# Routing the row tiles of a fused retention and mixture-of-experts kernel in groups of six instead of four or five

## The chip, the cores and the metric

The kernel runs on one core of one Trainium2 chip. The time is that of one execution on the device, in microseconds. The core has a matrix engine (TensorE, PE), a vector engine (VectorE, DVE), an activation engine (ScalarE, ACT), GpSimd (POOL) and a queue engine (SyncE, SP). Each works through its own instructions in order, and they wait for each other through semaphores.

## The reference, cut to what matters

```python
scores = (1/8) * q @ k.T                     # 8 batches x 8 heads x 576 x 64
x = (scores * decay_mask) @ v                # -> 4608 rows of 512
# first mixture layer
logits = x @ w_gate
e_idx  = argmax(logits, axis=1)              # one of 8 experts for each row
gate_w = softmax(logits)[e_idx]
eom    = sigmoid(x @ w_output_gate)[e_idx]
y[row] = gate_w * eom * (relu(x @ w1[e_idx]) @ w2[e_idx])
# second mixture layer: the same on y, with a bias by modality in the logits and no eom
```

## The kernel before, in words

The kernel has two parts. The first part (`attention_and_routing`, up to about 283 us of the profiled execution) computes the retention and the routing of the first mixture layer. The second part (`experts`, the rest) runs both expert layers; no line of it is touched.

The 4608 rows are cut into 36 row tiles of 128 rows. Nine tiles belong to a pair of batches: four chunks of each batch, and a "tail" tile (the ninth) made of the last 64 rows of both. Each tile is an object `Chunk` with some 30 parts: splits of q, k and v into a high and a low half (lines 308 to 341), scores (line 343), masks on POOL or DVE (line 360), the state of the recurrence (lines 371 to 390), products with the state (`qS`, line 407) and with v (`av`, line 425), the scaled output (`out`, line 429), the sum of squares (line 433), scales from its exponent (`row_scale` and `row_scale2`, lines 440 to 446), the row in two halves (lines 448 to 453), its DMA transpose (line 455), and the logits (line 457), which PE writes for each tile into its own 64 columns of a PSUM bank that the group shares.

The routing is done once for a group of tiles, in the generator `route` (line 207): a chain of small DVE instructions over all tiles of the group (sum of the logits' three parts, the product with the scale `iv`, maximum, one-hot choice `oh`, running counts `pre`, softmax denominators, positions `pi`), with two exponentials on ACT and two matmuls on PE between them. One step of the generator is issued at a time. After the last step `scatter` (line 201) writes each tile's rows to DRAM with an indirect DMA that POOL issues. The groups before are the tiles 0 to 3, 4 to 8, 9 to 12, 13 to 17, 18 to 21, 22 to 26, 27 to 30, 31 to 34 and 35: nine groups, eight of four or five tiles and one of a single tile.

The order of the work is written out by hand. Each part of tile i has a due time i + `PLAN[part]` in units of a tile (about 7 us in the middle of this part). The steps of a group's `route` follow the due time of its last logits at 0.1684 units each, its scatters come 0.225 units after the last step and 0.428 units apart, and 16 conversions of the first expert's weights (line 545, one ACT and one DVE instruction each) are due at the times in `WEIGHTS`. All of it is sorted by due time, and that is the order of each engine's instructions. Due times say nothing of the real time: an engine starts its next instruction when what it waits for is there.

Where the last group's chain has its place is read from the same numbers: its last logits are due at 34 + 5.707 = 39.707, its 21 steps end at 43.243, and the single tile's chain ends at 44.257. Weight conversions are due at 39.36, 39.38, 39.68, 39.83, 43.38, 44.04, 44.13, 45.14 and later.

The first part ends with a drain (the trace puts it on line 1434): SP waits for the scatters' data to land, and then all engines go on to the experts.

Of the kernel before, what the change touches and what calls it, by code (L numbers as in the profile page):

```python
# [11 lines left out]
F16 = mybir.dt.float16  # L12
BF16 = mybir.dt.bfloat16
F32 = mybir.dt.float32
I32 = mybir.dt.int32
AF = mybir.ActivationFunctionType
ALU = mybir.AluOpType
AX = mybir.AxisListType

B, H, S, HD = 8, 8, 576, 64  # L20
D, F, E = 512, 1024, 8
N = B * S
P = 128
# [4 lines left out]
XW = 512 + XM  # L28
# [4 lines left out]
NT = N // P  # L33
# [21 lines left out]
    "mh1": (1.231, 1.362, 1.017, 0.873, 1.420),  # L55
    "ml1": (1.412, 1.539, 1.052, 1.300, 1.605),
    "av1": (2.106, 1.795, 1.790, 1.802, 2.282),
    "qS1": (-8.214, 2.045, 1.567, 1.937, 1.514),
    "out": (2.400, 2.098, 1.999, 2.210, 2.465),
    "sq": (2.541, 2.150, 3.296, 2.949, 2.775),  # L60
    "rs1": (2.976, 2.479, 3.923, 3.559, 3.293),
# [6 lines left out]
FIRST = -3.462, -0.341, 0.344, 0.159, -0.039  # L68
GATES = -5.2, -1.440, -2.415, 1.091
WARM = 15  # L70
STEPS, STEP, LATE, SLACK = 21, 0.1684, 14, 1
SCATTER = 0.225, 0.428
WEIGHTS = 39.36, 39.38, 39.68, 39.83, 43.38, 44.04, 44.13, 45.14, 52.52, 59.82, 70.32, 70.53, 71.67, 73.74, 109.54, 132.91

# [36 lines left out]
def attention_and_routing(tc, st, I, K):  # L111
# [3 lines left out]
    one, two, three = pool("one", 1), pool("two", 2), pool("three", 3)  # L115
# [72 lines left out]
    class Group:  # L188


        def __init__(self, start, items):
            self.tag, self.items, self.G, self.start = start, items, len(items), start
            tag = start
            for i, x in enumerate(items):
                x.group, x.place = self, i
            s1 = lambda n, dt=F32: two.tile([P, 5], dt, bufs=3, tag=n, name=f"{n}{tag}")
            self.ss, self.eb, self.sc, self.iv = s1("ss"), s1("eb", I32), s1("sc"), s1("iv")
            self.xrow = two.tile([P, 5, XW], F32, bufs=3, tag="xr", name=f"xr{tag}")
            self.pm = None

    def scatter(x):
# [5 lines left out]
    def route(gr):  # L207

        v, G, tag, pm, sc, iv = nc.vector, gr.G, gr.tag, gr.pm, gr.sc, gr.iv
        sm = lambda w, n, dt=F32: two.tile([P, 5, w], dt, tag=n, name=f"{n}{tag}")  # L210
        s1 = lambda n, dt=F32: two.tile([P, 5], dt, tag=n, name=f"{n}{tag}")
        g = slice(0, G)
        bc = lambda a, w: a[:, g].unsqueeze(2).to_broadcast([P, G, w])
        lg, dl, ex, wq, oh = sm(16, "lg"), sm(8, "dl"), sm(8, "ex"), sm(8, "wq"), sm(8, "oh", F16)
        mx, se, m2 = s1("mx"), s1("se"), s1("m2")
        v.tensor_reduce(lg[:, g], pm[:, 0:64 * G].rearrange("p (g c) -> p g c", c=64)[:, :, 0:48].rearrange("p g (s e) -> p g e s", s=3), axis=AX.X, op=ALU.add)
        yield
        v.tensor_tensor(lg[:, g], lg[:, g], bc(iv, 16), op=ALU.mult)
        yield
        v.tensor_reduce(mx[:, g], lg[:, g, 0:8], axis=AX.X, op=ALU.max)  # L220
        yield
        v.tensor_tensor(dl[:, g], lg[:, g, 0:8], bc(mx, 8), op=ALU.subtract)
        yield
        desc = col("desc").unsqueeze(1).to_broadcast([P, G, 8])
        v.scalar_tensor_tensor(wq[:, g], dl[:, g], 0.0, desc, op0=ALU.is_ge, op1=ALU.mult)
        yield
        v.tensor_reduce(m2[:, g], wq[:, g], axis=AX.X, op=ALU.max)
        yield
        v.tensor_tensor(oh[:, g], wq[:, g], bc(m2, 8), op=ALU.is_ge)
        nc.scalar.activation(ex[:, g], dl[:, g], AF.Exp)  # L230
        yield

        pre = two.tile([P, 6, 8], F16, tag="pre", name=f"pre{tag}")
        v.tensor_copy(pre[:, 0], cum[0])
        for t in range(5):
            if t < G:
                v.tensor_tensor(pre[:, t + 1], pre[:, t], oh[:, t], op=ALU.add)
            yield
        cum[0] = pre[:, G]
        zz, pr = sm(8, "zz"), sm(8, "pr")  # L240
        z, en, pf, pi = s1("z"), s1("en"), s1("pf"), s1("pi", I32)
        v.tensor_tensor(zz[:, g], lg[:, g, 8:16], oh[:, g], op=ALU.mult)
        yield
        v.tensor_reduce(z[:, g], zz[:, g], axis=AX.X, op=ALU.add)
        yield
        v.tensor_reduce(se[:, g], ex[:, g], axis=AX.X, op=ALU.add)

        o = pm[:, 320:320 + 8 * G]
        nc.tensor.matmul(o, tri, oh[:, g, :], start=True, stop=False)
        nc.tensor.matmul(o, ones, pre[:, g, :], start=False, stop=True)  # L250
        yield
        v.tensor_scalar(se[:, g], se[:, g], 1e-9, None, op0=ALU.add)
        nc.scalar.activation(en[:, g], z[:, g], AF.Exp, scale=-1.0)
        yield
        meta = gr.xrow[:, g, 512:XW]
        t0 = gr.items[0].row
        v.tensor_copy(meta[:, :, 1:XM], tokm[:, t0:t0 + G, :])
        yield
        v.tensor_tensor(pr[:, g], o.rearrange("p (g e) -> p g e", e=8), oh[:, g], op=ALU.mult)
        yield  # L260
        v.tensor_reduce(pf[:, g], pr[:, g], axis=AX.X, op=ALU.add)
        yield

        v.scalar_tensor_tensor(en[:, g], en[:, g], 1.0, se[:, g], op0=ALU.add, op1=ALU.mult)
        yield
        v.tensor_copy(pi[:, g], pf[:, g])
        v.scalar_tensor_tensor(meta[:, :, 0], en[:, g], WS * WS, sc[:, g], op0=ALU.mult, op1=ALU.mult)
        gr.pi = pi
# [16 lines left out]
    class Chunk:  # L285
# [74 lines left out]
        def mask(self, r, part):  # L360

            src = (self.au, self.al)[part][r]
            dst = src if part else three.tile([P, 512], F16, bufs=3, tag="ah", name=f"ah{self.tag}_{r}")
            self.aa[r][part] = dst
            s4, d4 = (t_.rearrange("p (h i) -> p h i", h=4) for t_ in (src, dst))
            if self.tail or self.on(("mh1", "ml1")[part]) is nc.vector:
                nc.vector.tensor_tensor(d4, s4, self.causal(), op=ALU.mult)
            else:
                nc.gpsimd.affine_select(out=d4, in_=s4, pattern=[[0, 4], [1, C]], compare_op=ALU.is_ge, fill=0.0, base=0, channel_multiplier=-1)
# [73 lines left out]
        def row_scale2(self):  # L443
            v = nc.vector
            v.tensor_scalar(self.of("sc").bitcast(I32), self.of("eb"), -8388608.0, 195.0 * 8388608.0, op0=ALU.mult, op1=ALU.add)
            v.tensor_scalar(self.of("iv").bitcast(I32), self.of("eb"), 8388608.0, 59.0 * 8388608.0, op0=ALU.mult, op1=ALU.add)

        def x_hi(self):
            self.xr = self.group.xrow[:, self.place, 0:512].bitcast(F16)
# [16 lines left out]
        order += [Chunk(2 * bp + bb, c) for bb in range(2) for c in range(NCH)] + [Chunk(2 * bp, NCH)]  # L466
    for i, x in enumerate(order):
        x.before = [order[i - 5], order[i - 1]] if x.tail else [order[i - 1]] if x.c else []
    cuts = [0] + [x + 9 * bp for bp in range(B // 2) for x in (4, 9)]
    cuts.insert(-1, NT - 1)  # L470
    groups = [Group(a, order[a:z]) for a, z in zip(cuts, cuts[1:])]
    whole = lambda f: lambda x: None if x.tail else f(x)
    parts = {
# [24 lines left out]
    for gr in groups:  # L498
        last = max(gr.start + n + PLAN["lg"][x.c] for n, x in enumerate(gr.items))
        chain = route(gr)  # L500
        for k in range(STEPS):
            last += STEP if k != LATE else STEP * SLACK
            add(last, next, chain, None)
        for n, x in enumerate(gr.items):
            add(last + SCATTER[0] + n * SCATTER[1], scatter, x)
# [13 lines left out]
    pm = ps.tile([P, 512], F32, tag="pl", bufs=2, name="pm_cnt")  # L519
# [901 lines left out]
def build(nc, I, off, outs):  # L1421
    with ExitStack() as st:
        sb = lambda n, s, dt: st.enter_context(nc.sbuf_tensor(n, s, dt))[:]
        K = {"off": off}
        K["cst"] = sb("cst", [P, max(b for _, b in off.values())], F32)
        K["ones"], K["tri"] = sb("ones", [P, P], F16), sb("tri", [P, P], F16)
        K["wg2"] = sb("wg2", [P, 4, 24], BF16)
        K["bias"] = sb("bias", [P, 16], F32)
        K["reg1"] = sb("reg1", [1, 24], I32)
        K["zero"] = sb("zero", [P, XW], F32)  # L1430
        K["wb0"] = sb("wb0", [P, 2, 8192], F16)
        K["xs1"] = nc.dram_tensor("xs1", [E * R, XW], F32, kind="Internal").ap()
        K["xs2"] = nc.dram_tensor("xs2", [E * R, XW2], F32, kind="Internal").ap()
        with tile.TileContext(nc) as tc, ExitStack() as s2:
            attention_and_routing(tc, s2, I, K)
        experts(nc, st, I, K, outs[0])
# [46 lines left out]
```

## Time and profile before

| | |
|---|---|
| median of three runs | 1137.59 us |
| the three runs | 1138.03, 1137.59, 1132.46 us |
| profiled execution, its own time | 1131.96 us |
| its span, first to last instruction | 1130.2 us |
| granted TensorE clock, mean over the span | 0.924 of full speed |
| busy: PE, DVE, ACT, POOL | 1025.8, 579.8, 439.8, 338.2 us |

The span is cut by the page into 40 slices, with the busy share of each engine in tenths (9 is 90% or more) and the clock that TensorE was granted:

```profile
PE   8897788880799999999999999999999999999996
...
DVE  7799999986455555555555565532412111111111
...
PEclk8858787865899999999999999999999999999999
```

A slice is 28.3 us, so the first part is the first ten slices. The rows of the views that go deeper stand in the section on rows below. In a timeline's row the first number is the start, the second the duration, and a bracket holds the idle time before it and what ended it.

### The profile page before, as it was taken

The page shows a single profiled execution, that of the slowest core. Times are in us where ns is not written, and L with a number is a line of the kernel's source. Part 1 is how long each engine was busy: PE and PEld are TensorE (multiplying, and loading weights), DVE is VectorE, ACT ScalarE, POOL GpSimd, SP SyncE. Part 2 cuts the span into 40 slices and gives each one's busy share as a digit, 9 for nine tenths or more (in the row PEclk, how much of TensorE's full clock was granted, in tenths as well). Part 3 has the DMA queues.
Part 4 walks back from the last instruction along what each step waited for, and adds up shares of the span by engine and source line. Part 5 has one row for each costly group of instructions (what it writes and reads, how often), then busy time and mean ns, then how long its engine had stood idle before and what let it go on. Part 6 is the DMA issues. An engine that isn't in the chain of part 4 may idle for free. (4 is left out here: it accounts for less than half of the span.)

```text
span 1130.2 us, 27289 instructions
## 1 busy us (share of the span) xinstructions
PE 1025.8 (91%) x10037; PEld 736.6 (65%) x10037; DVE 579.8 (51%) x1624; ACT 439.8 (39%) x833; POOL 338.2 (30%) x370
## 2 busy tenths in 40 slices
PE   8897788880799999999999999999999999999996
PEld 6786677770566767576666566667676667667664
DVE  7799999986455555555555565532412111111111
ACT  7767666743243434343434434323311111111111
POOL 7868788755112121212211121220110111011010
PEclk8858787865899999999999999999999999999999
DMA  8557677764666566657467455627211121221200
GB/s 297 136 146 188 189 199 199 176 198 126 228 187 149 143 147 151 139 141 144 141 174 172 78 159 128 150 61 208 67 48 45 48 67 40 54 50 47 56 28 31
DMA packets 213056, 145.07 MB, mean 128 GB/s; under 512 B 174089, under 2 KB 174253, under 8 KB 212912
## 3 DMA queue, kind: packets, MB, share of 16 engines
q1 hardware_dynamic: 203952, 114.63, 41.6%
q0 software_dynamic: 8960, 28.62, 7.2%
q8 instruction: 79, 1.29, 0.5%
q14 instruction: 65, 0.53, 0.2%
HBM read 70.75 MB, written 33.92 MB: 93 GB/s over the span
## 5 line engine op out<-in xcount | busy, mean ns | idle before, releaser
L1062 PE MATMUL ph<-xT,wb 128*128 128x256 f16 (+2 forms) x1344 | 338.7, 263 | 22.5 <-PEq L566 22.5
L1064 PE MATMUL ph<-xT,wb 128*128 128x256 f16 (+2 forms) x1344 | 338.8, 263 | 0.0
L1063 PE MATMUL ph<-xT,wb 128*128 128x256 f16 (+2 forms) x1344 | 338.7, 263 | 0.0
L1270 DVE SCALAR_TENSOR_TENSOR hT<-ph,hT 128x512 f16<-128x512 f32 (+2 forms) x168 | 106.5, 638 | 333.3 <-DVEq L566 332.4
L1070 PE MATMUL py<-wb,hT 128*128 128x512 f16 x608 | 231.0, 380 | 1.4 <-PEq L566 0.7
L1071 PE MATMUL py<-wb,hT 128*128 128x512 f16 x608 | 231.1, 380 | 0.0
L1072 PE MATMUL py<-wb,hT 128*128 128x512 f16 x608 | 230.9, 380 | 0.0
L1161 ACT ACTIVATE hT<-ph 128x512 f16<-128x512 f32 (+2 forms) x168 | 93.0, 553 | 225.4 <-ACTq L566 225.3
L1062 PEld LDWEIGHTS ph<-xT,wb 128*128 128x128 f16 x1344 | 131.6, 98 | 40.3 <-issue 23.3
L1063 PEld LDWEIGHTS ph<-xT,wb 128*128 128x128 f16 x1344 | 131.6, 98 | 16.9
L1064 PEld LDWEIGHTS ph<-xT,wb 128*128 128x128 f16 x1344 | 131.6, 98 | 12.9
L1388 POOL DMA_INDIRECT out_dram<-yo,idxo x37 | 35.9, 972 | 333.4 <-POOLq L566 330.1
L1377 POOL TENSOR_SCALAR idx<-v_pos 128x1 int32<-128x1 f32 x39 | 15.5, 397 | 337.7 <-POOLq L566 337.7
L1072 PEld LDWEIGHTS py<-wb,hT 128*128 128x128 f16 x608 | 59.6, 98 | 72.3 <-issue 0.8
L1070 PEld LDWEIGHTS py<-wb,hT 128*128 128x128 f16 x608 | 59.5, 98 | 67.4 <-issue 2.5
L1071 PEld LDWEIGHTS py<-wb,hT 128*128 128x128 f16 x608 | 59.5, 98 | 65.2 <-issue 0.6
L1155 ACT ACTIVATE yo<-py,v_gcol 128x512 f32<-128x512 f32 x37 | 25.4, 687 | 169.0 <-ACTq L566 169.0
L578 DVE SCALAR_TENSOR_TENSOR wb<-stg,wb 128x2048 f16<-128x2048 f32 x36 | 82.5, 2291 | 11.0 <-DVEq L566 11.0
L1138 ACT ACTIVATE wb<-stg 128x2048 f16<-128x2048 f32 x36 | 68.5, 1901 | 0.0
L1149 ACT ACTIVATE sq<-py 128x512 bf16<-128x512 f32 x39 | 23.3, 597 | 113.9 <-ACTq L566 113.9
L1381 POOL DMA_INDIRECT xs<-x2row,idx x39 | 50.3, 1290 | 37.5 <-POOLq L566 37.5
L350 PE MATMUL pa<-qT,kT 64*128 64x128 f16 x864 | 43.9, 260 | 18.1 <-DVE al L279 17.7
(175 smaller groups left out, 1439.2 us busy)
## 6 DMA issues: line engine op xcount, KB each, us to landing
stg<-in_moe_w_dram SPq DMA_DIRECT2D x36, 1024.0 KB, 5.7
kn<-in_k_dram SPq DMA_DIRECT2D x36, 256.0 KB, 3.9
qn<-in_q_dram SPq DMA_DIRECT2D x36, 256.0 KB, 4.2
vn<-in_v_dram SPq DMA_DIRECT2D x36, 256.0 KB, 5.0
w0s<-in_moe_w_dram SPq DMA_DIRECT2D x16, 256.0 KB, 4.4
xs<-zero SPq DMA_DIRECT2D x8, 262.0 KB, 2.9
xs<-zero SPq DMA_DIRECT2D x8, 258.0 KB, 2.5
xT<-xs SPq DMA_TRANSPOSE x42, 4.3
```

The source lines that it names most:

```text
L350: nc.tensor.matmul(self.pa[r][:, hp * P:(hp + 1) * P], self.kT[HALF[r], 4 * x + hp, :], self.qT[HALF[r], y, hp, :], start=(n == 0), stop=( ...
L578: r = fn(*a, **kw).then_inc(self.sem, 1)
L1062: pe.matmul(o, w1(P_, 0)[:, c, fs], xT[s][:, c, cs], start=(c == 0), stop=False)
L1063: pe.matmul(o, w1(P_, 0)[:, c, fs], xT[s][:, 4 + c, cs], start=False, stop=False)
L1064: m = pe.matmul(o, w1(P_, 1)[:, c, fs], xT[s][:, c, cs], start=False, stop=(c == 3))
L1070: pe.matmul(py[b], hT[:, 0, f, bs], w2(P_, 0)[:, f, :], start=(f == 0), stop=False)
L1071: pe.matmul(py[b], hT[:, 0, f, bs], w2(P_, 1)[:, f, :], start=False, stop=False)
L1072: m = pe.matmul(py[b], hT[:, 1, f, bs], w2(P_, 0)[:, f, :], start=False, stop=(f == 7))
L1138: ac.activation(wb[P_ % 2][:, 0, 2048 * c:2048 * c + 2048], stg[:, 2048 * c:2048 * c + 2048], AF.Copy, scale=WS).then_inc(T["cv_full"])
L1161: ac.activation(hT[:, 0, 2 * g:2 * g + 2, cs], ph[g][:, :, cs], AF.Relu).then_inc(T["hh_full"])
L1270: stt(hT[:, 1, 2 * g:2 * g + 2, cs], ph[g][:, :, cs], 0.0, hT[:, 0, 2 * g:2 * g + 2, cs], op0=ALU.max, op1=ALU.subtract).then_inc(T["h_full"])
L1381: po.indirect_dma_start(out=xs2, out_offset=bass.IndirectOffsetOnAxis(ap=idx[b], axis=0), in_=x, in_offset=None, bounds_check=E * R - 1, o ...
```

## The change

The tiles are grouped by six: tiles 0 to 5, 6 to 11, 12 to 17, 18 to 23, 24 to 29, 30 to 34 and 35. That makes seven groups: five of six tiles, one of five, one of one. The generator has a loop over six tiles instead of five, so a chain has 22 steps instead of 21. The scale `iv` of the logits is computed from the exponents with one instruction for the group, in the second step of `route`, instead of one instruction for each tile in `row_scale2`. Tiles of SBUF that hold a group's data get six places, and the buffers of the masked high half `ah` go from three to two. The part `qS1` of a tail tile moves from 1.514 to 2.283, which is just behind `av1` of the same tile (2.282). The constants `LATE` and `SLACK` go; with `SLACK` = 1 they did nothing. The core of the diff:

```diff
-    "qS1": (-8.214, 2.045, 1.567, 1.937, 1.514),
+    "qS1": (-8.214, 2.045, 1.567, 1.937, 2.283),
...
-STEPS, STEP, LATE, SLACK = 21, 0.1684, 14, 1
+TILES = 6
+STEPS, STEP = 16 + TILES, 0.1684
...
-            self.xrow = two.tile([P, 5, XW], F32, bufs=3, tag="xr", name=f"xr{tag}")
+            self.xrow = two.tile([P, TILES, XW], F32, bufs=3, tag="xr", name=f"xr{tag}")
...
         v.tensor_reduce(lg[:, g], pm[:, 0:64 * G]...
         yield
+        v.tensor_scalar(iv[:, g].bitcast(I32), gr.eb[:, g], 8388608.0, 59.0 * 8388608.0, op0=ALU.mult, op1=ALU.add)
         v.tensor_tensor(lg[:, g], lg[:, g], bc(iv, 16), op=ALU.mult)
...
-        for t in range(5):
+        for t in range(TILES):
             if t < G:
                 v.tensor_tensor(pre[:, t + 1], pre[:, t], oh[:, t], op=ALU.add)
             yield
...
-        o = pm[:, 320:320 + 8 * G]
+        o = pm[:, 64 * TILES:64 * TILES + 8 * G]
...
-            dst = src if part else three.tile([P, 512], F16, bufs=3, tag="ah", name=f"ah{self.tag}_{r}")
+            dst = src if part else three.tile([P, 512], F16, bufs=2, tag="ah", name=f"ah{self.tag}_{r}")
...
             v.tensor_scalar(self.of("sc").bitcast(I32), self.of("eb"), -8388608.0, 195.0 * 8388608.0, op0=ALU.mult, op1=ALU.add)
-            v.tensor_scalar(self.of("iv").bitcast(I32), self.of("eb"), 8388608.0, 59.0 * 8388608.0, op0=ALU.mult, op1=ALU.add)
...
-    cuts = [0] + [x + 9 * bp for bp in range(B // 2) for x in (4, 9)]
-    cuts.insert(-1, NT - 1)
+    cuts = [*range(0, NT - TILES + 1, TILES), NT - 1, NT]
...
-            last += STEP if k != LATE else STEP * SLACK
+            last += STEP
```

## Rows read from the trace of the kernel before

**Rows 1.** Busy time by stretch: start:end, length, busy us (instructions), clock, DMA
```profile
80.00:240.00 160.00, 131.06 (x2454) 115.08 (x2454) 154.43 (x349) 107.91 (x217) 126.64 (x130) 0.78 0.74 193
240.00:283.00 43.00, 15.24 (x244) 13.13 (x239) 29.93 (x118) 16.71 (x37) 23.10 (x18) 0.54 0.52 143
283.00:1130.00 847.00, 810.39 (x6258) 550.51 (x6258) 328.50 (x1021) 259.30 (x478) 128.53 (x155) 0.99 0.43 109
```
**Rows 2.** Waits, 80 to 240 us: total, times, longest
```profile
PE pa L350 <- DVE al L279: 14.1, 7, 3.7
...
DVE a L420 <- PE pa L350: 5.0, 10, 1.9
```
**Rows 3.** Instructions by line, DVE, 60 to 300 us: count, busy us, mean ns
```profile
L229 DVE TENSOR_TENSOR oh<-wq,m 128x32 f16<-128x32 f32 (+2 forms) x9 | 11.3, 1260 | 0.1
...
L264 DVE SCALAR_TENSOR_TENSOR en<-en,se 128x4 f32<-128x4 f32 (+2 forms) x9 | 4.1, 452 | 0.0
L257 DVE COPY xr<-tokm 128x44 f32<-128x44 f32 (+2 forms) x9 | 3.8, 421 | 0.0
...
L252 DVE TENSOR_SCALAR se<-se 128x4 f32<-128x4 f32 (+2 forms) x9 | 3.4, 374 | 0.0
...
L216 DVE TENSOR_REDUCE lg<-pl 128x64 f32<-128x192 f32 (+2 forms) x9 | 3.1, 348 | 2.5 <-PE pl L462 1.5 <-PE pl L249 0.9
...
L218 DVE TENSOR_TENSOR lg<-lg,iv 128x64 f32<-128x64 f32 (+2 forms) x9 | 3.1, 344 | 0.1
L242 DVE TENSOR_TENSOR zz<-lg,oh 128x32 f32<-128x32 f32 (+2 forms) x9 | 2.7, 296 | 0.0
...
L222 DVE TENSOR_TENSOR dl<-lg,mx 128x32 f32<-128x32 f32 (+2 forms) x9 | 1.7, 187 | 0.1
...
L267 DVE SCALAR_TENSOR_TENSOR xr<-en,sc 128x4 f32<-128x4 f32 (+2 forms) x9 | 1.4, 153 | 0.0
```
**Rows 4.** DVE timeline around 131 us, in the third group's chain
```profile
131.28 4.31 DVE L229 TENSOR_TENSOR oh<-wq,m 128x32 f16<-128x32 f32 x1
...
135.85 0.15 DVE L445 TENSOR_SCALAR sc<-eb 128x1 int32<-128x1 int32 x1
135.91 0.14 DVE L446 TENSOR_SCALAR iv<-eb 128x1 int32<-128x1 int32 x1
135.97 0.15 DVE L237 TENSOR_TENSOR pre<-pre,oh 128x8 f16<-128x8 f16 x1
136.05 0.74 DVE L453 SCALAR_TENSOR_TENSOR xr<-xg,sc,xr 128x512 f16<-128x512 f32 x1
```
**Rows 5.** POOL timeline, same stretch: first and last of five
```profile
131.19 0.65 POOL L369 TENSOR_SCALAR_AFFINE_SELECT ah<-au 128x512 f16<-128x512 f16 x1
...
134.50 1.03 POOL L317 TENSOR_TENSOR vs<-vn,cst 128x512 f32<-128x512 f32 x1
```
**Rows 6.** PE timeline, first tail tile: its qS1, end of its av1
```profile
66.30 1.30 PE L404 MATMUL po<-Sh,qT 64*64 64x64 f16 x24
...
73.14 0.24 PE L404 MATMUL po<-vh,al 128*128 128x64 f16 x1
```
**Rows 7.** DVE timeline, first tail tile: its out
```profile
75.14 0.68 DVE L431 TENSOR_TENSOR xg<-po,cst 128x512 f32<-128x512 f32 x1
```
**Rows 8.** POOL timeline, the last scatters of the first part
```profile
266.74 1.25 POOL L203 DMA_INDIRECT xs<-xr,pi  x1 [3.45 <-DVE se L246]
...
269.96 5.24 POOL L203 DMA_INDIRECT xs<-xr,pi  x1 [0.30 <-ACT wb L547]
275.51 0.98 POOL L203 DMA_INDIRECT xs<-xr,pi  x1 [0.30 <-issue]
276.79 0.98 POOL L203 DMA_INDIRECT xs<-xr,pi  x1 [0.30 <-issue]
```
**Rows 9.** DVE timeline beside them: nine weight conversions in one run
```profile
268.85 5.50 DVE L548 SCALAR_TENSOR_TENSOR wb<-w0s,wb 128x512 f16<-128x512 f32 x9
```
**Rows 10.** Waits of SP's queue, 237 to 300 us: total, times, longest
```profile
SPq L1434 <- DMA xs<-xr,pi: 20.0, 3, 8.6
```

## What the change is expected to do

> **What bounds the kernel now.** I read the busy shares in 40 slices first: there are two parts, and only the first, up to 283 us, contains lines that change. The busy times by stretch come next [rows 1]. From 283 us on PE is busy 810.4 of 847 us at a clock of 0.99; nothing there changes, the rows reach DRAM in the same order whatever the groups are, and I carry that part over unchanged. From 80 to 240 us DVE is busy 154.4 of 160 us (97%), PE 131.1 and POOL 126.6. The waits confirm that DVE sets the pace [rows 2]: PE stands 14.1 us for DVE's residuals, DVE only 5.0 us for PE's scores. So a DVE instruction that goes saves time there; one that is added costs it. From 240 to 283 us DVE is busy 29.9 of 43 us and the end is set by something else: SP waits for scatters to land [rows 10], POOL issues the last at 276.79 [rows 8]. A scatter added behind it costs its full time.
>
> In the DVE-bound stretch the instructions by line show a second thing [rows 3]. A group's chain has 18 DVE instructions besides one `pre` sum for each tile. Eleven of them last between 0.153 and 0.187 us on average (the two ends are shown), but six last 0.30 to 1.26 us. The timeline shows why [rows 4, 5]: the `oh` of line 229 lasts 4.31 us, 131.28 to 135.59, exactly while POOL works through five instructions without a gap, 131.19 to 135.53. DVE was held until POOL paused. Two such rows of 4.31 us make 8.6 of line 229's 11.3 us.
>
> **Part by part, against the profiled execution (1131.96 us, span 1130.2 us).**
>
> *Two groups fewer.* The sums over a group have the same elements for each tile, so what goes is the fixed price of two chains. Mean price: 1.260 + 0.452 + 0.421 + 0.374 + 0.344 + 0.296 = 3.15 us, plus 0.35 (line 216), plus 11 x 0.17 = 1.87, together 5.4 us [rows 3]. Small instructions overlap: those of rows 4 are reported 0.14 to 0.15 us long and start 0.06 apart, so about 0.08 of each is no cost, 18 x 0.08 = 1.4. That leaves 3.9 us a group. Floor, if the waits for POOL stay: all 18 at 0.17 and 0.18 more for line 216 is 3.2, less 1.4, makes 1.8. By due times, the groups whose chains lie in the DVE-bound stretch go from six to four; the chains that end on tiles 11 and 17 keep their places to a hundredth of a unit, and so does the chain that ends on tile 29 or 30, which belongs to the end. One of the chains that vanish (tiles 18 to 21) holds one of the two 4.31 us rows; with that row whole it is worth 3.9 + (4.31 - 1.26) = 7.0 us. So two groups are worth 3.6 us (2 x 1.8) to 10.9 us (3.9 + 7.0). A vanished instruction does not take its whole wait with it: line 453, with two SBUF inputs like line 229, stands only five instructions further on [rows 4] and would meet the rest of the same POOL run. I take about half the way from floor to mean, 3.0 each: **-6.0**.
>
> *One `iv` for a group.* Line 446 costs 0.06 us from start to start [rows 4]. 25 of its 36 copies lie between 70 and 237 us: -1.5. Four grouped ones are added there, as the first thing of the second step, in front of the product that needs it. The trace has no such instruction on several columns; the lower bound is line 446's own 0.06 us, the upper line 252's 0.374, also one input and several columns. I take 0.12, nearer the row of the same operation and type: +0.5. Together **-1.0**, between -1.3 and 0.
>
> What the profile shows of line 252 bears on the second bound [rows 3]: one input, five columns at most, and yet twice the duration of the undisturbed ones. The Trainium skill (GPSIMD Engine Reference, Specifications) says that POOL shares its SBUF interfaces with DVE, and that they collide for DVE instructions with two SBUF inputs or in a mode that uses both ports. By line 446's rows the grouped `iv` is free of that, and the term is -1.3; by the page's rule it may be held like line 252, and the term is 0; it cannot be settled from this trace.
>
> *`qS1` of the tail behind `av1`.* 24 matmuls, 1.30 us at the low clock [rows 6], move between `av1` and `out`. `out` is a DVE instruction with the whole of DVE's queue behind it. For the first tail, `av1` ends at 73.38 [rows 6] and `out` starts at 75.14 [rows 7]: 1.76 us of room, more than 1.30, so DVE does not notice. For the third group's tail the room is longer only because of the 4.31 us row. If such a wait goes, DVE is at `out` early and pays up to 1.3 us; the last tail has this order already. Zero to 3.9 us for three tails, and I take **+0.5**, near the row with room. PE gives the same 1.3 us back earlier, where it waits for DVE anyway [rows 2].
>
> *`ah` in two buffers.* A buffer is written again two tiles later; by due times 0.6 units or more (some 4 us) lie between `av1` reading it and POOL's next write. Nothing, with that room as cover; without it POOL would stand and the masks would be late.
>
> *The end.* The last full group has five tiles instead of four: one more scatter behind the chain, 1.28 us from start to start [rows 8]. Its chain has a step more, so its last step is due at 43.41 instead of 43.24 and falls behind the weight conversion due at 43.38: 0.61 us on DVE (5.50 / 9) [rows 9], with a `pre` sum and an `iv` some 0.2 to 0.3 more. The scatters thus start about 0.9 us later. The third scatter is held for 5.24 us while DVE runs nine conversions [rows 8, 9]; it ends when these end, so part of the 0.9 is hidden if again two scatters come before the run, and one scatter more falls behind it if not. Bounds: 1.3 (delay hidden) and 1.28 + 0.9 + 1.28 = 3.5. I take **+2.2**. The six scatters of tiles 24 to 29, two more than stand there now, fit into POOL's 3.45 us of idle time [rows 8] at 2 x 1.28 = 2.6; without that cover they would add to the end too.
>
> *Sum:* -6.0 - 1.0 + 0.5 + 2.2 = -4.3 us: 1131.96 becomes 1127.7. The runs shown lie at 1132.5 and, twice, 1138; the profiled one is like the lowest. Against the median, 1137.59 - 4.3 = 1133.3, rounded to **1133**. A difference under 0.5% (5.7 us) can't be told from no change with this kernel.
>
> **The rivals.**
>
> *The waits go with the groups.* If nothing catches the vanished waits, two groups are worth 7.8 (2 x 3.9) to 10.9, say 9.4, `iv` 1.3, the end costs 2.0: -8.7, **1129**. For it: the two rows of 4.31 us sit at the same step of two chains, and one chain goes. Against: POOL's 126.6 us of work remain, and other DVE instructions with two SBUF inputs come all the time.
>
> *The gain is swallowed.* PE is busy 131 of 160 us at a clock of 0.78 [rows 1], and POOL 127; where these bind locally, shortening DVE buys less. Floor for the groups (3.6) less a third for PE, -2.4, `iv` 0, end +2.4: **1137.6**. Against: DVE stood only 5.0 us for PE [rows 2].
>
> *New holds (slower).* Two of the four chains (ending on tiles 5 and 23) have new places, and the grouped `iv` is a new instruction in each. If `oh` or `iv` falls to a POOL run like that of rows 5, DVE loses 4.2 us (4.31 - 0.1) each time, and PE with it. From the second such run on the sum is above zero; with two, and the end at 3.5 us, it is -4.3 + 8.4 + 1.3 = +5.4; with a third it is +9.6. I name **1144**, between them +6.4. For it: two of the six chains meet such a run today. Against: runs of five POOL instructions are few, and holds of this length move with the whole schedule.
>
> **How the numbers follow.** Forecast 0.47, its own range -9 to +1 (1128.6 to 1138.6); waits go 0.25; swallowed 0.15; new holds 0.13. Faster by over 0.5%: a third of the forecast (0.16) and nearly all of the second (0.24), 0.40. Slower: most of the last (0.12) and a little of the third (0.02), 0.14. Same: 0.46. For the range I take the low run with the second case's far end, 1132.5 - 9.5 = 1123, and the high run with half of the last case, 1138 + 3 = 1141.
>
> **What would show each step.** Right: seven rows each for lines 216 to 267, seven for line 446's instruction instead of 36, the last `out` of line 431 some 6 to 7 us earlier, the last scatter only 4 to 5 us earlier, POOL's last scatter some 2 us further behind the last logits than now. Wrong: rows of line 229, or of the new `iv`, over 2 us in the chains on tiles 5 and 23; idle time of line 431 on PE; POOL waiting before line 369 on `ah`; or a change of the second part's 847 us by more than 2 us, which would mean that I placed the effect in the wrong part.

## The result: the changed kernel is slower, and part of the loss lies in the first part

The changed kernel takes 1142.67 us (median of 9 runs, 1139.0 to 1149.0), the kernel before 1134.12 us (9 runs beside them, 1129.38 to 1138.66): ratio 1.0087, 95% interval 1.0059 to 1.0114. The forecast was 1133 us, and 1142.67 lies outside its range of 1123 to 1141. The profiled execution took 1142.67 us, span 1140.9; that of before 1131.96 and 1130.2. As a difference the forecast was -4.3 us, and the medians differ by +8.6. Part of the distance from 1133 to 1142.67 has nothing to do with the change: the forecast started from 1137.59 us, the median of three runs, and nine runs have 1134.12. Two executions below of some 1224 us, at a clock of 0.81 where the others have 0.91 to 0.94, belong to a slower state of the chip and are in no ratio.

How finely such a ratio can be read is shown by the kernel before, run against itself: 1.0026, interval 1.0000 to 1.0052. Measured again, the changed kernel came to 1143.53 us, 1.0095 (1.0057 to 1.0132). The comparison of a kernel with itself is called the null comparison here. Against it the change loses some 0.6 to 0.7%, 7 to 8 us.

Busy time by stretch of the changed kernel, cut where its second part begins (as [rows 1]: length, then busy us of PE, PEld, DVE, ACT, POOL, then clock and DMA):

```profile
80.00:240.00 160.00, 130.81 (x2358) 114.81 (x2353) 146.05 (x296) 103.92 (x206) 118.80 (x122) 0.75 0.65 177
240.00:288.00 48.00, 19.88 (x321) 16.80 (x317) 33.44 (x128) 20.25 (x45) 26.27 (x25) 0.60 0.63 181
288.00:1140.00 852.00, 812.61 (x6258) 551.77 (x6258) 328.30 (x1021) 259.37 (x478) 129.35 (x155) 0.98 0.44 109
```

The reader is to see that DVE fell from 154.43 to 146.05 of 160 us: in the same length of time it stood idle 8.4 us more. The waits of DVE in the same stretch say for what (as [rows 2], DVE's alone, all but a last one of 0.6; before had the one row of 5.0):

```profile
DVE a L422 <- PE pa L352: 3.6, 8, 0.6
DVE Sn L385 <- PE pS L381: 2.9, 5, 0.7
DVE xg L433 <- PE po L406: 1.9, 2, 1.7
DVE a L422 <- issue: 1.8, 1, 1.8
DVE Sn L385 <- PE pS L379: 1.3, 2, 0.8
DVE xg L433 <- issue: 1.1, 1, 1.1
```

For scores (L422) DVE waits 5.4 us, about as long as before; new are the waits for the state (`Sn`, L385, 4.2 us) and for `out` (`xg`, L433, 3.0 us). The longest of these is at `out` of a tail, the third, at 205.67; but one of 1.07 us is at `out` of tile 21, which is no tail, and of the state's 4.2 us only 1.1 come directly behind `out` of a tail. The first tail lies just ahead of the stretch. Here is `out` of the first and of the third tail and the first one's state on DVE, then PE around the first tail [rows 6, 7]:

```profile
73.35 0.69 DVE L433 TENSOR_TENSOR xg<-po,cst 128x512 f32<-128x512 f32 x1 [1.37 <-PE po L406]
...
75.11 0.42 DVE L385 TENSOR_TENSOR Sn<-pS,cst 128x256 f32<-128x256 f32 x1 [1.01 <-PE pS L381]
...
205.67 0.69 DVE L433 TENSOR_TENSOR xg<-po,cst 128x512 f32<-128x512 f32 x1 [1.68 <-PE po L406]
```
```profile
69.90 1.43 PE L352 MATMUL pa<-qT,kT 64*128 64x128 f16 x23 [2.99 <-DVE eb L443]
...
72.02 1.30 PE L406 MATMUL po<-Sh,qT 64*64 64x64 f16 x24
73.25 0.50 PE L463 MATMUL pl<-wg,xT 128*128 128x48 bf16 x8
```

PE stands 2.99 us, runs the scores that it waited for, `av1`, then `qS1` for 1.30 us at a granted clock of 0.50 (the lower level, 1.2 GHz), and DVE, already there, waits 1.37 us for it. In the kernel before, `qS1` ran at 66.30, ahead of that wait of PE, which was 0.70 us there, and DVE came to `out` with room.

The chains did get shorter. DVE's lines from 60 to 300 us [rows 3], now seven of each; longest means first, with some of the others:

```profile
L224 DVE TENSOR_TENSOR dl<-lg,mx 128x48 f32<-128x48 f32 (+2 forms) x7 | 4.6, 658 | 0.1
...
L259 DVE COPY xr<-tokm 128x66 f32<-128x66 f32 (+2 forms) x7 | 3.7, 528 | 0.0
L219 DVE TENSOR_SCALAR iv<-eb 128x6 int32<-128x6 int32 (+2 forms) x7 | 3.3, 477 | 0.0
...
L217 DVE TENSOR_REDUCE lg<-pl 128x96 f32<-128x288 f32 (+2 forms) x7 | 2.9, 410 | 3.1 <-PE pl L463 3.1
...
L254 DVE TENSOR_SCALAR se<-se 128x6 f32<-128x6 f32 (+2 forms) x7 | 2.3, 335 | 0.1
...
L231 DVE TENSOR_TENSOR oh<-wq,m 128x48 f16<-128x48 f32 (+2 forms) x7 | 1.8, 264 | 0.1
...
L266 DVE SCALAR_TENSOR_TENSOR en<-en,se 128x6 f32<-128x6 f32 (+2 forms) x7 | 1.3, 179 | 0.0
```

All lines of the chains together (L216 to L267 before, L217 to L269 now) fell from 57.9 to 48.0 us. The `oh` instruction fell from 11.3 to 1.8; the rows of 4.31 us are gone. Other rows got longer: `dl` (L224) rose from 1.7 to 4.6 us with one row of 2.23 us, and the grouped `iv`, 3.3 of the 48.0, has rows of 1.05 us (shown at the end).

The end of the first part on POOL [rows 8], then DVE's conversions beside it [rows 9] and SP's wait for scatters, once and 6.1 us where it was 20.0 in three times [rows 10]:

```profile
265.80 1.78 POOL L204 DMA_INDIRECT xs<-xr,pi  x1 [11.06 <-DVE xr L269]
...
278.67 1.50 POOL L204 DMA_INDIRECT xs<-xr,pi  x1 [0.31 <-ACT wb L547]
280.48 1.50 POOL L204 DMA_INDIRECT xs<-xr,pi  x1 [0.30 <-issue]
282.28 0.98 POOL L204 DMA_INDIRECT xs<-xr,pi  x1 [0.30 <-issue]
288.20 3.52 POOL L1393 MEMSET hT<- 128x4096 f16 x1 [4.94 <-issue]
```
```profile
276.23 5.49 DVE L548 SCALAR_TENSOR_TENSOR wb<-w0s,wb 128x512 f16<-128x512 f32 x9
```
```profile
SPq L1434 <- DMA xs<-xr,pi: 6.1, 1, 6.1
```

Three marks divide the first part, read off the timelines of DVE and POOL: the last tile's `out`, the last scatter, and POOL's MEMSET of `hT`, with which the second part begins.

| profile of | last `out` | last scatter | MEMSET | from there to the end |
|---|---|---|---|---|
| before | 253.47 | 276.79 | 283.32 | 846.9 |
| before, again | 253.35 | 276.64 | 283.15 | 849.1 |
| changed | 259.78 | 282.28 | 288.20 | 852.7 |
| changed, again | 262.09 | 284.48 | 290.40 | 851.4 |

The first part is 4.9 and 7.2 us longer. The second part, which does not change, took between 842.8 and 853.2 us in the eight profiles of whole kernels made here, so the 5.8 us between the first and the third row can't be put down to the change. But the first part does not hold the whole loss either. These two profiles are of the median runs, whose times lie 8.6 and 10.7 us above the medians of before, so 3 to 4 us lie behind the first part in both.

### The profile page after: what moved, and what is told of

It is laid out like the page before. It is cut to its first block, busy times and chain, and to the rows that moved or that the text cites. A ratio compares the mean times of both kernels' runs of the same rounds, so it can differ in the third digit from the quotient of the medians.

```text
span 1140.9 us, 27182 instructions
## 1 busy us (share of the span) xinstructions
PE 1031.1 (90%) x10033; PEld 739.2 (65%) x10033; DVE 573.0 (50%) x1559; ACT 439.3 (39%) x829; POOL 335.7 (29%) x370
## 5 line engine op out<-in xcount | busy, mean ns | idle before, releaser
L1377 POOL TENSOR_SCALAR idx<-v_pos 128x1 int32<-128x1 f32 x39 | 12.1, 311 | 342.7 <-POOLq L566 342.7
L1149 ACT ACTIVATE sq<-py 128x512 bf16<-128x512 f32 x39 | 23.3, 597 | 114.5 <-ACTq L566 114.5
```

## The experiments

Theory: the loss is the late `qS1` of the tails, which stands in front of DVE's waits. Rivals: the six-tile groups bring new holds; the grouped `iv` is held; the second part changes. In the expectations Q stands for the theory, G for the groups, S for the second part; the distances are those from one tail's `out` to the next, first to second and second to third.

**Whole kernels.** The change's parts, one at a time (here and below a line of `-` is the kernel named, `+` the experiment). Before with the late `qS1`:

```
-    "qS1": (-8.214, 2.045, 1.567, 1.937, 1.514),
+    "qS1": (-8.214, 2.045, 1.567, 1.937, 2.283),
```


> The kernel before with one number changed: qS1 of a tail tile due at 2.283 instead of 1.514. Theory Q (the late qS1 of the tail is what costs): the distance from one tail's out to the next grows from 62.2 and 62.0 us to about 66, as in the changed kernel (66.1, 66.2), and the time rises by 5 to 10 us against before. Theory G (the groups of six cost): the distances stay within 0.5 us of 62.2 and 62.0, and the time is that of before within 2 us. Theory S (the second part's own scatter from run to run makes the difference): first part as before, time anywhere between 1129 and 1139.

1133.54 against 1131.54 us, ratio 1.0022 (0.9986 to 1.0058).

The changed kernel with `qS1` of the tail at 1.600 instead of 2.283:

> The changed kernel with qS1 of a tail due at 1.600, near its old place, instead of 2.283. Theory Q: the distances between the tails' outs fall from 66.1 and 66.2 us to 62 or less, and the time is some 5 to 10 us under the changed kernel, so at or up to 4 us under that of before. Theory G: the distances stay near 66 and the time stays some 8 us over before. Theory S: no difference in the first part beyond 1 us.

1135.24 us, 1.0041 (1.0013 to 1.0070).

Before with one `iv` for each group (the line goes from `row_scale2` to `route`, as in the change):

> The kernel before with iv made once for a group in the second step of route, everything else as before. My prediction's term says -1.0 us (-1.3 to 0). Theory Q and theory G both expect the time of before within 2 us. A theory V (the grouped iv is held by POOL and sets the pace back): +2 to +6 us, with rows of the new instruction over 1 us.

1133.74 us, 1.0023 (0.9993 to 1.0053).

Groups of six alone, with `ah` in two buffers, `iv` for each tile, and `qS1` at 1.600:

> Groups of six (and two buffers of ah), with iv made for each tile as before and qS1 of a tail at 1.600. Theory Q: the time of before less about 3 us (my -6.0 for two groups, +2.2 at the end), distances between tails' outs 62 or less. Theory G: 5 to 10 us over before, distances near 66.

1134.85 us, 1.0033 (1.0005 to 1.0061).

The null comparison and the changed kernel again, whose results the section above has:

> The kernel before itself, unchanged, as one of the kernels compared: what the comparison shows where nothing differs. Ratio 1.000 within 0.3%; its profile gives a second length of the part behind the first (846.9 us in the profile that I have). Theory S1 (that part scatters by itself by some 10 us from run to run, whatever the kernel): this profile's value lies anywhere in 842 to 854. Theory S2 (that part is longer behind groups of six): here it stays near 847 or below.

> The changed kernel itself once more, beside the kernel before in the same call. The first time it was 1.0087 of before, 9.9 us, of which its first part alone explains 3.6 (288.5 against 284.9). Theory S1: the ratio falls towards 1.003 (3.6 us). Theory S2: it stays near 1.009, so some 6 us lie behind the first part.

What follows: none of the four can be told from the null's 1.0026, the changed kernel can. With groups of six, moving `qS1` back takes the ratio from 1.0087 and 1.0095 to 1.0041; that points at the late `qS1` together with the groups, but the intervals of 1.0041 and 1.0087 overlap. Late `qS1` on the groups of before shows no loss. The scatter of the second part hides anything smaller.

The distances that the expectations named fit neither Q nor G. They are 62.2 and 62.0 us before, 66.1 and 66.2 in the changed kernel (67.5 and 65.2 again), and 63.8 and 62.5, 65.8 and 63.2, 63.5 and 63.2 for late `qS1` alone, `qS1` at 1.600 and groups alone: groups of six and the late `qS1` both stretch them.

The changed kernel's second measurement was to decide whether anything lies behind the first part, and its ratio stayed at 1.0095, which its expectation had as some 6 us there. The next experiments give the first parts: by the medians the changed kernel loses 3.6 us in its first part alone and 8.6 and 10.7 whole; with `qS1` at 1.600 its first part is 2.7 us shorter than before and the whole kernel 3.7 longer, and groups alone have 2.1 shorter and 3.3 longer. In each of these four comparisons the whole kernel does 5 to 7 us worse than its first part alone. The null has 3.7 us with nothing changed, and the profiles' second parts are 843.3 to 853.2 us behind groups of six and 842.8 to 850.5 behind the others. What this is stays open; the experiments below can't see it.

**The first part alone.** The second part was cut off to get rid of that scatter:

```
-        experts(nc, st, I, K, outs[0])
+            nc.sync.dma_start(outs[0][0:P, :], K["zero"][:, 0:512])
```

> The first part of the kernel before alone: the experts are left out, and 128 rows of zeros are written to the output in their place. It ends at 283.3 us in the profile of the whole kernel, so about 285 us here, and its runs show how far the first part alone scatters. Theory F (the first part makes the difference): scatter under 1 us, so that differences of 1 us between the four kernels of this kind can be read. Theory S (the loss lies in the second part): the four agree within 2 us.

> The first part of the changed kernel alone (experts left out, zeros written to 128 rows). Theory F: 5 us over the same part of before, as in the two profiles (288.2 against 283.3), or more, up to 10 us if it explains the whole loss. Theory S: within 2 us of it.

> The first part alone of the changed kernel with the tail's qS1 due at 1.600. Theory Q (the late qS1 costs, together with the groups): 4 us under the changed one's first part, as in the profiles (284.2 against 288.2). If qS1 is without effect: the same within 1 us.

> The first part alone with groups of six, iv for each tile and the tail's qS1 at 1.600. The profile of the whole kernel says 279.8 us, 3.5 under before: if that holds, the groups by themselves are worth what I forecast for them less the end, and the grouped iv costs 4 us in this schedule (284.2 against 279.8). If the single profile was luck: within 1 us of the kernel with the grouped iv.

These four ran on one chip: before 284.9 us (284.53 to 285.25), changed 288.49 (287.47 to 288.78), changed with `qS1` at 1.600 282.23 (four runs 281.96 to 283.56, one 289.05), groups alone 282.8 (281.44 to 284.52). So the groups gain 2.1, the grouped `iv` 0.6, and the late `qS1` costs 6.3: together +3.6. That four first parts differ by more than 2 us speaks against the second part as the only place of the loss. Busy time from 70 to 230 us, before, then changed, then changed with `qS1` at 1.600:

```profile
70.00:230.00 160.00, 131.26 (x2413) 115.31 (x2406) 153.67 (x349) 108.24 (x215) 127.96 (x132) 0.76 0.71 190
```
```profile
70.00:230.00 160.00, 135.10 (x2321) 119.17 (x2317) 144.83 (x288) 104.26 (x204) 118.32 (x121) 0.70 0.65 174
```
```profile
70.00:230.00 160.00, 129.64 (x2384) 114.23 (x2380) 148.67 (x301) 106.96 (x211) 122.38 (x126) 0.76 0.70 181
```

DVE's waits there, changed and then with `qS1` at 1.600; before had 5.2 us for scores and 0.4 more:

```profile
DVE a L422 <- PE pa L352: 6.6, 11, 2.3
DVE xg L433 <- PE po L406: 4.2, 5, 1.6
DVE Sn L385 <- PE pS L381: 3.2, 5, 1.0
DVE Sn L385 <- PE pS L379: 0.4, 1, 0.4
```
```profile
DVE a L422 <- PE pa L352: 6.5, 9, 1.8
DVE Sn L385 <- PE pS L381: 1.5, 3, 0.9
DVE xg L433 <- PE po L406: 1.3, 2, 1.1
DVE Sn L385 <- PE pS L379: 1.2, 2, 0.8
```

The waits for `out` and the state go from 7.8 us (4.2 + 3.2 + 0.4) to 4.0 (1.3, and 2.7 for `Sn`); that is 3.8 us, 2.9 of them at `out`. The first and the third tail pay at `out`, 1.37 and 1.64 us, with `qS1` at 1.600 none and 0.14; the second tail waits in neither. The rest is seen in DVE's own time. The spans of these two profiles are 287.1 and 281.8 us, and DVE's 538 instructions, the same in both, are busy 2.4 us longer in the first (first lines of the pages, changed, then `qS1` at 1.600); why is not shown:

```profile
PE 219.5 (76%) x3775; PEld 188.9 (66%) x3775; DVE 245.5 (86%) x538; ACT 180.0 (63%) x351; POOL 206.2 (72%) x215
```
```profile
PE 213.3 (76%) x3775; PEld 183.6 (65%) x3775; DVE 243.1 (86%) x538; ACT 179.8 (64%) x351; POOL 206.7 (73%) x215
```

The granted clock is a rival: 0.70 from 70 to 230 us in the changed kernel, 0.76 with `qS1` at 1.600, and PE is busy 5.5 us longer there.

The two single parts on the groups of before, on another chip:

> The first part alone (experts left out, zeros written to 128 rows) of the kernel before with qS1 of a tail at 2.283. Theory Q alone (the late qS1 costs by itself): 3 to 6 us over the first part of before, 288 to 291. Theory QG (it costs only with the groups of six, where it took 6.3 us: 288.5 against 282.2): within 1 us of 284.9.

> The first part alone (experts left out, zeros written to 128 rows) of the kernel before with iv made once for a group. My term: -1.0 us (-1.3 to 0), so 283.9 against 284.9. With the groups of six the grouped iv came to -0.6 (282.2 against 282.8). A hold by POOL would make it 286 or more.

Late `qS1` 289.6 us (four runs, 286.2 to 292.41), +4.7; grouped `iv` 285.43 (284.39 to 287.77), +0.5, both against the first part of before on the other chip. The first contradicts the whole kernel with the same edit, whose last `out` came at 250.18 us, where this one's profile, of its longest run, has 261.83. Whether late `qS1` also costs with groups of four and five stays open. One thing is the same in both profiles: DVE stands at `out` of none of the first three tails, and then up to 0.47 us for the state. The first tail of the whole kernel, without a wait:

```profile
73.61 0.68 DVE L431 TENSOR_TENSOR xg<-po,cst 128x512 f32<-128x512 f32 x1
```

**Where `qS1` costs, and whether DVE sets the pace.**

> First part alone (the experts are left out). The changed kernel with the tail's `qS1` at 2.281, directly ahead of `av1` (2.282) instead of directly behind it; all else of TensorE's order as in the changed kernel. Beside 288.5 us (changed, 2.283) and 282.2 us (1.600). If the cost is that `out` waits for the 24 matmuls that stand behind `av1`, they now run before it, and most of the 6.3 us comes back: 283 to 285. If it is that the 24 matmuls come late in TensorE's order at all, whichever side of `av1`, nothing comes back: 287 to 289.

> First part alone (the experts are left out). The changed kernel with the tail's `qS1` at 1.900, half-way between 1.600 (282.2 us) and 2.283 (288.5). A cost that grows with lateness gives about 285; one that comes only with the place directly ahead of `out` gives 282 to 283.

> First part alone (the experts are left out). The changed kernel, `qS1` at 2.283, with the tail's `out` due at 2.620 instead of 2.465, so that VectorE has other work of about one microsecond between `av1`'s end and `out`. If the stall of VectorE at `out` (4.2 us in the profile of the changed first part) is the price, it goes: 284 to 286. If the price is paid by TensorE's later order and lower clock, 288 to 289; if what follows `out` is then late instead, 289 or more.

> First part alone (the experts are left out). The kernel before, with the logits' scale `iv` written five times for each tile instead of once: 144 more tiny operations on VectorE, some 60 ns each or 8.6 us in all, with nothing added on another engine. Beside 284.9 us. If VectorE sets the pace throughout, +7 to +9: 292 to 294. If TensorE and the waits for it set most of the pace, +0 to +3: 285 to 288, and then work taken from VectorE gains as little.

- At 2.281, ahead of `av1`: 289.36 us (286.72 to 293.98). In the whole nothing comes back, so the place behind `av1`, on which the prediction's term rested, does not make the price. Up to the last `out` the profile is 1.9 us shorter than that of 2.283; its end is 3.1 us longer, because a scatter is held there (last section). This also speaks against the rival of the clock: from 70 to 230 us it is 0.75 here, PE is busy 131.0 us, nearly as with `qS1` at 1.600, and the span is 288.7 us all the same.
- At 1.900: 283.5 us (281.09 to 285.32), between its two expectations.
- `out` later: 292.62 us (291.07 to 293.96). DVE's idle time at `out` fell to 1.9 us, but `Sn` behind it waited 8.8 us, and the kernel got slower. A stall at `out` is not removed by arriving later.
- `iv` five times: 303.35 us (300.8 to 307.04), +18.5 against before on another chip; both expectations were too low. Five in a row take 0.89 us, each starting 0.19 us after the last, where independent ones start 0.06 apart. The row of DVE's timeline, then the first lines of the pages of before, of groups alone and of this one:

```profile
120.64 0.89 DVE L447 TENSOR_SCALAR iv<-eb 128x1 int32<-128x1 int32 x5
```
```profile
PE 209.2 (74%) x3779; PEld 180.0 (64%) x3779; DVE 250.0 (88%) x603; ACT 180.0 (64%) x355; POOL 210.1 (74%) x215
```
```profile
PE 215.9 (77%) x3775; PEld 184.8 (66%) x3775; DVE 245.8 (88%) x567; ACT 179.8 (64%) x351; POOL 206.5 (74%) x215
```
```profile
PE 230.4 (75%) x3779; PEld 200.6 (66%) x3779; DVE 272.1 (89%) x747; ACT 180.6 (59%) x355; POOL 205.5 (67%) x215
```

DVE's busy time rose by 22.1 us. The profile is of the longest run, whose span is 21.9 us over that of before; the medians differ by 18.5. So work added to DVE does cost, most of its length or all of it. Groups of six took 4.2 us off and gained 2.1, half of it.

Last, the two places directly on either side of the scores for which PE waits:

> First part alone (the experts are left out). The changed kernel with the tail's `qS1` at 2.170: directly ahead of the scores of the second tile after the tail (2.181), for which TensorE stands 2 to 4 us waiting on VectorE's residuals `al`. If the price comes from standing behind that wait, there is none yet: 282 to 285, as at 1.600 (282.2) and 1.900 (283.5). If it grows with the distance, nearly all of it is there: 287 to 289.

> First part alone (the experts are left out). As the last, but `qS1` at 2.190: on TensorE only its 24 matmuls and the 24 of those scores change places, for three tails. If the price comes from standing behind the wait that those scores have, all of it comes at this step: 287 to 290, as at 2.281 (289.4) and 2.283 (288.5), some 5 us above 2.170. If it comes with the distance, the two differ by less than 1 us.

285.54 us (283.5 to 285.93) and 287.7 us (283.93 to 291.12). PE around the second tail, at 2.170 and at 2.190:

```profile
131.37 1.30 PE L406 MATMUL po<-Sh,qT 64*64 64x64 f16 x24
...
134.27 1.43 PE L352 MATMUL pa<-qT,kT 64*128 64x128 f16 x23 [1.38 <-DVE al L281]
```
```profile
132.91 1.44 PE L352 MATMUL pa<-qT,kT 64*128 64x128 f16 x23 [3.86 <-DVE al L281]
134.28 1.30 PE L406 MATMUL po<-Sh,qT 64*64 64x64 f16 x24
```

The exchange is as meant: at 2.170 `qS1` runs in the time that PE would stand anyway, and the wait shrinks to 1.38; at 2.190 PE stands 3.86 us and runs `qS1` after it. But the step is 2.2 us, with overlapping runs, and both expectations fail. In the profiles the last `out` is 1.4 us later (255.51 against 254.09); the rest of that pair's 4.5 us came at the end, where one scatter was held (next section).

All places together, groups of six, first part alone, medians:

| `qS1` at | 1.600 | 1.900 | 2.170 | 2.190 | 2.281 | 2.283 |
|---|---|---|---|---|---|---|
| us | 282.2 | 283.5 | 285.5 | 287.7 | 289.4 | 288.5 |
| last `out` in the profile | 254.3 | 255.7 | 254.1 | 255.5 | 257.6 | 259.5 |
| clock, whole span | 0.748 | 0.730 | 0.745 | 0.757 | 0.749 | 0.725 |

The price rises with the distance, by some 6 us over it; no single exchange holds it. Ahead of PE's wait all three are below 286, behind it all three above 287. Not all of this is one price: in the profiles of 2.190 and 2.281 some 3 us come from the held scatter at the end, and up to the last `out` those two lie 1.2 and 3.3 us above 1.600, and 2.283 lies 5.2 above it. The columns come from three chips, and the profile of 1.900 is of its longest run, so differences of 1 to 2 us between neighbours are not to be read.

## Why the prediction was wrong, step by step

**`qS1` behind `av1`: +0.5, bounds 0 to 3.9. This is the step that failed.** It was worth +6.3 us with groups of six in the first part alone. Its reasoning was that `av1` ended 1.76 us before `out` in the first tail, more than 1.30. Two things were wrong in that. The room was taken as fixed, though it was the lateness of DVE; the same change shortened DVE's chains, so DVE comes to `out` early and waits (1.37 us at 73.35, 1.68 at 205.67). The prediction named this case ("DVE is at `out` early and pays up to 1.3 us") and took +0.5 all the same, near the tail with room. That the groups, and not `qS1` alone, make DVE early fits the kernel with late `qS1` on the groups of before, whole and first part alone, where DVE stood at `out` of none of the first three tails. And `out` was taken for the only reader, while the state stands behind `qS1` too; but this is the smaller error, for DVE waits for `Sn` behind the tails' `out` also with `qS1` at 1.600 (0.30, 0 and 0.92 us, against 1.01, 0.36 and 0.74), and the late `qS1` adds 0.9 us to all waits for the state. The sentence "PE gives the same 1.3 us back earlier, where it waits for DVE anyway" was a true observation read the wrong way: since PE waits there anyway, nothing is given back. That `qS1` had been covered by that wait is what the move lost: at the first tail PE stands 0.70 us before and 2.99 after. The bound of 3.9 counted 1.30 us for each of three tails at `out`, and nothing that stands behind `qS1` on PE. Shown: the size with groups of six, that the side of `av1` does not make it, and that `qS1` shortens PE's wait when it stands ahead of it. Of the price, 2.9 us are waits at `out` of two tails, 0.9 waits for the state, and 2.4 longer instructions of DVE, in one pair of profiles. Not settled: why those got longer, and why the kernel with late `qS1` on the groups of before is 4.7 us over before in its first part without any wait at the tails' `out`.

**Two groups fewer: -6.0, bounds -3.6 to -10.9.** Mis-sized: -2.1 us with everything that the groups bring, the end among it, where -6.0 and +2.2 make -3.8. Up to the last `out` it is 1.15 us (253.34 against 254.49). The 4.31 us holds went; but in the first part alone DVE's busy time fell by 4.2 us only, and its waits for PE rose from 5.6 to 7.5 us (4.0 scores, 2.6 state, 0.9 `out`). That DVE binds was right for added work. For work taken away DVE's waits for PE took back 1.9 of the 4.2 us, which the rival "the gain is swallowed" had, and which the mean prices of rows 3 could not show.

**One `iv` for a group: -1.0.** -0.6 with groups of six, +0.5 on the groups of before: none that can be told from nothing.

**`ah` in two buffers: 0.** In POOL's waits of the changed kernel line 371 (before line 369) waits 1.6 us for ACT's `au` where it writes `ah`, and never for PE, which reads the buffer; it was not run by itself.

**The end: +2.2.** From the last `out` to the last scatter the changed kernel takes 22.5 us (282.28 - 259.78), before 23.3: -0.8. All six scatters of tiles 24 to 29 start late, after 11.06 us of waiting for the chain, and run on without a gap into the last six; the hold of 5.24 us did not come. Where it comes with groups of six (`qS1` at 2.190 and 2.281), the end takes 25.7 and 25.6 us, +2.3: the forecast's size.

**The second part: unchanged.** Not shown. The prediction's own sign, a change of 847 us by more than 2, did appear (852.7 and 851.4), but the kernel before itself has 849.1 in its second profile, so the sign was set too fine for a part that scatters by 10 us. The terms above add up to +3.6 us, and the whole kernel lost 8.6 and 10.7: the other 5 to 7 us are accounted for by none of them, and the cause is open.

**Rivals.** "New holds", 1144 us, came nearest in time and is not the cause: no row of `oh` is over 0.69 us in the first profile (1.76 in the second) and none of `iv` over 1.05, and all lines of the chains together got shorter. The sign that did appear and pointed to the step that failed was one of the prediction's own: "idle time of line 431 on PE".

No version tried beats the kernel before as a whole: `qS1` at 1.600 and groups alone have first parts 2.7 and 2.1 us shorter and still ratios of 1.0041 and 1.0033, not better than the null.

## What to carry to other kernels

When a batch of matmuls is moved, look at which wait of its own engine it stood in front of: there the wait covered it, and behind the wait it stands in front of everything that the engine does next. Room before a consumer is the consumer's lateness; if the same change makes the consumer earlier, the room goes with it. Here work taken from the busiest engine was worth half of its length, while work added cost most of it, so a term for each needs its own measure. A null comparison should stand beside any claim under one per cent, and a part that can be cut out and timed alone should be added up with the rest before the whole difference is put down to it.

## What the runs showed of the hardware

A one-input DVE instruction lasts longer beside POOL too. The grouped `iv`, six columns, took 1.05 us and ended with POOL's instruction beside it (90.35 and 90.32); on DVE and on POOL of the changed kernel:

```profile
89.30 1.05 DVE L219 TENSOR_SCALAR iv<-eb 128x6 int32<-128x6 int32 x1
```
```profile
88.74 1.58 POOL L326 TENSOR_TENSOR vh<-vs,vh 128x512 f16<-128x512 f32 x1
```

The Trainium skill (GPSIMD Engine Reference, Specifications) has POOL and DVE collide for DVE instructions with two SBUF inputs or in a mode that uses both ports. `iv` has one input, so by that rule it would have to be in such a mode; the run shows the long row, not the mode. Of the line's seven rows, another of 1.05 and one of 0.60 us also end within 0.03 us of a POOL instruction (222.55 and 222.52, 127.12 and 127.09); the other four last 0.15 to 0.16 us.

A scatter on POOL can last 5.25 us beside DVE's run of nine conversions, or not. With `qS1` at 2.190, POOL and DVE:

```profile
273.05 5.25 POOL L204 DMA_INDIRECT xs<-xr,pi  x1 [0.30 <-issue]
```
```profile
271.95 5.49 DVE L548 SCALAR_TENSOR_TENSOR wb<-w0s,wb 128x512 f16<-128x512 f32 x9
```

In the changed kernel, beside the same run of 5.49 us from 276.23, no scatter took more than 1.50 us. The one that began 1.1 us after the run's start, as above, is this:

```profile
277.32 1.04 POOL L204 DMA_INDIRECT xs<-xr,pi  x1 [0.30 <-issue]
```

What decides is open, and it moves the end by 3 us.

The granted clock does not order the times: the whole span at 2.190 had 0.757 and took 286.3 us, at 2.170 0.745 and 281.8.
